# Feed-forward layers of a routed attention kernel: two batches at a time, by seven block products in place of eight

## The chip, the cores and the metric

The kernel runs on one core of one Trainium2 chip. The metric is the device time in microseconds of one execution; the time before is the median of three runs. The engines of a core are named as the profile names them: PE is the matrix engine (PEld its weight loads), ACT the scalar engine, DVE the vector engine, POOL the GpSimd engine, and SP the queue from which most transfers are issued.

## The reference

First an attention block with pooled queries, over 8 batches of 8 heads, 1152 keys and 64 elements per head. Then, per batch, a gate scores each of the 576 pooled tokens, the best 128 go through a feed-forward network (FFN) of 512 to 1024 to 512, and its output is added to those tokens, weighted by the gate. Everything is in 32-bit floats.

```python
def _attn_ref(q, k, v):                       # q, k, v: (8, 8, 1152, 64)
    q_pool = q.reshape(B, H, S // 2, 2, D).mean(axis=3)
    scores = scale * np.matmul(q_pool, k.transpose(0, 1, 3, 2))
    scores = scores - np.max(scores, axis=-1, keepdims=True)
    attn = np.exp(scores)
    attn = attn / (np.sum(attn, axis=-1, keepdims=True) + 1e-09)
    return np.matmul(attn, v)

def _moe_ref(x, w_gate, w1, w2, capacity):    # x: (8, 576, 512), capacity 128
    scores = np.einsum('bsd,d->bs', x, w_gate)
    out = x.copy()
    for b in range(B):
        top_idx = np.argpartition(-scores[b], capacity)[:capacity]
        xe = x[b, top_idx]
        h = np.maximum(xe @ w1, 0.0)          # w1: (512, 1024)
        ye = h @ w2                           # w2: (1024, 512)
        g = 1.0 / (1.0 + np.exp(-scores[b, top_idx]))
        out[b, top_idx] = x[b, top_idx] + g[:, None] * ye
    return out
```

## The kernel before

The program is a loop over 64 halves: 8 batches, 4 pairs of heads each, and every pair's 576 queries in two halves of 288. In half `h` the PE makes the scores of `h` and then the weighted values of `h - 1`; ACT takes the exponentials out of PSUM; POOL and DVE fold their sums, transpose, normalize and gate.

```python
def scores(self, half):
    ...
    for c in range(self.NC):                       # 9 blocks of keys
        sc = self.banks()                          # one of 4 PSUM tiles of 2 banks
        for e in range(2):
            for j in range(2):
                nc.tensor.matmul(sc[keys, j, 0:n], lhsT=pair["kT"][...], rhs=pair["qT"][rows, qs], ...)  # L818
        nc.scalar.activation(p[:, c // G, c % G, :, :], sc[:, :, 0:n], AF.Exp, scale=self.scale)         # L825

def weighted(self, half):
    av = self.banks()
    ...     nc.tensor.matmul(av[...], lhsT=half["pair"]["v"][keys, j, c, :], rhs=half["p"][...], ...)    # L836
    nc.scalar.copy(two[:, :, :], av[:, :, 0:n])                                                          # L844
    nc.gpsimd.tensor_tensor(out=half["av"][:, :], in0=two[:, 0, :], in1=two[:, 1, :], op=ALU.add)        # L846

def folded(self, half):
    acc = self.work.tile([P, G, 2 * self.HALF], F32, name="acc")
    for u in range(G):
        nc.gpsimd.tensor_tensor(out=acc[:, u, :], in0=units[:, 0, u, :], in1=units[:, 1, u, :], op=ALU.add)  # L857
    for a, of in enumerate((units[:, 2, :, :], acc[:, :, :])):
        nc.vector.tensor_reduce(fold[:, a, :], ..., apply_transpose=True)                                # L862
    nc.vector.tensor_reduce(pair["sum"][:, :, ns], fold..., AX.X, ALU.add)                               # L872
```

When a batch's four pairs are done, a generator `routed` does the gate and the FFN of that batch in small steps. What a step yields says at which of three places of a half the next one is put: "mid" (between the scores and the weighted values), "sums" (after the folding) or the end of the half. `gated` makes the last product with the gate's weights and starts it.

```python
def gated(self, half):
    ...
    nc.vector.tensor_reduce(pair["red"][:, ns], pair["prod"][:, ns, :], AX.X, ALU.add)
    if half["s"] == 1:
        engine.tensor_tensor(out=pair["part"][...], in0=pair["red"], in1=pair["rec"], op=ALU.mult)       # L986
        if pair["hp"] == self.NPAIR - 1:
            self.routing.append([pair["b"], self.routed(pair["b"], pair["part"]), "sums"])

def routed(self, b, part):
    nc.vector.tensor_reduce(line[:, :], part..., AX.X, ALU.add)                                          # L1010
    ...   # batch 6: nc.tensor.matmul(ps, lhsT=merge, rhs=line)                                           # L1024
    ...   # scores to a row in DRAM and back, ranks on DVE, ranks to DRAM and back
    for of, to in ((self.token_line, found), (lines[:, :, 1, :], own_gate)):
        nc.vector.scalar_tensor_tensor(out=pick..., in0=lines[0:w, :, 0, :], scalar=token, in1=of, ...)  # L1169
    nc.gpsimd.indirect_dma_start(out=xe[0:w, :], in_=rows_out, ...)                                      # L1188
    ...
    for c in range(self.ND):                        # 4 blocks of 128
        nc.tensor.transpose(pv[:, c, 0:w], xe[0:w, c * P : (c + 1) * P], ident)                          # L1205
    nc.scalar.copy(xeT[:, :, 0:w], pv[:, 0 : self.ND, 0:w])                                              # L1208
    yield mid
    for f0 in range(0, self.NFC, 4):                # 8 blocks of 128 hidden units
        pv = self.banks()[:, 0, :]...
        for f in range(4):
            for c in range(self.ND):
                nc.tensor.matmul(pv[:, f, 0:w], lhsT=self.w1[:, c, ...], rhs=xeT[:, c, 0:w], ...)        # L1216
            if f == 3:
                nc.scalar.activation(hT[:, f0 : f0 + 4, 0:w], pv[:, :, 0:w], AF.Relu)                    # L1224
            yield "hidden" if f0 + f == self.NFC - 1 else False
    ps = self.banks()[:, 0, :]
    for f in range(self.NFC):
        nc.tensor.matmul(ps[0:w, 0:512], lhsT=hT[:, f, 0:w], rhs=self.w2[:, f, :], ...)                  # L1229
        yield False
    nc.scalar.activation(y[0:w, :], ps[0:w, 0:512], AF.Copy, scale=own_gate[0:w, 0:1])                   # L1248
    nc.gpsimd.tensor_tensor(out=xe[0:w, :], in0=y[0:w, :], in1=xe[0:w, :], op=ALU.add)                   # L1253
    nc.gpsimd.indirect_dma_start(out=rows_out, in_=xe[0:w, :], ...)                                      # L1254
```

So the FFN of one batch is 32 matmuls of 128 x 128 by 128 and 8 of 128 x 128 by 512. The layers of batch 5 (second one), 6 and 7 run after the loop, in an order written out by hand, where they fill the waits of batch 7's own chain of gate, ranks and gather.

Buffers: `kb`, `qb`, `kT`, `qT`, `prod`, `sc_row` 2 each, `v_sb` 3. Loads of a pair are issued from SP one pair ahead.

Of the kernel before, what the change touches and what calls it, by code (L numbers as in the profile page):

```python
# [10 lines left out]
P = 128  # L11
# [523 lines left out]
class _Plain:  # L535
# [10 lines left out]
    def __init__(self, ctx, tc, q, k, v, moe_w_gate, moe_w1, moe_w2, capacity, out):  # L546
# [27 lines left out]
        assert 0 < self.TAIL < P and self.Dm == self.ND * P and self.Dm <= 512  # L574
        assert self.F == self.NFC * P and self.NFC % 4 == 0
# [17 lines left out]
        self.w2 = self.const.tile([P, self.NFC, self.Dm], F32, name="w2")  # L593

# [21 lines left out]
    def constants(self):  # L616
# [13 lines left out]
        slot_i = self.ffn.tile([P, self.Sp], I32, name="cmp", bufs=1)  # L630
        nc.gpsimd.iota(slot_i[:, :], pattern=[[1, self.Sp]], base=0, channel_multiplier=0)
        self.slot_f = const.tile([P, self.Sp], F32, name="slot_f")
        nc.vector.tensor_copy(self.slot_f[:, :], slot_i[:, :])
# [34 lines left out]
    def line_of_scores(self):  # L668

        line = self.ffn.tile([P, self.NT * P], F32, name="sc_row")  # L670
        self.nc.gpsimd.memset(line[0:1, self.Sp :], 0.0)
        return line
# [16 lines left out]
    def weight_loads(self):  # L689

        w1 = self.w1_in.rearrange("(c p) f -> p c f", p=P)
        w2 = self.w2_in.rearrange("(c p) d -> p c d", p=P)
        for c in range(self.ND):
            yield self.nc.sync.dma_start(self.w1[:, c, :], w1[:, c, :])
        for c in range(0, self.NFC, 2):
            yield self.nc.sync.dma_start(self.w2[:, c : c + 2, :], w2[:, c : c + 2, :])
# [3 lines left out]
    def load_pair(self, b, hp):  # L700
# [3 lines left out]
        qb = self.load.tile([P, self.QB, 2, BLK], F32, name="qb")  # L704
# [8 lines left out]
    def load_values(self, pair):  # L713


        nc, hp = self.nc, pair["hp"]
        v_sb = pair["v"] = self.load.tile([P, 2, self.NC, self.D], F32, name="v_sb", bufs=3)
        of = self.v[pair["b"], 2 * hp : 2 * hp + 2]
        of = of.rearrange("j (i g c) d -> g i j c d", i=BLK, c=self.NC)
        for g in range(P // BLK):  # L720
            nc.sync.dma_start(
                v_sb[g * BLK : (g + 1) * BLK, :, :, :].rearrange("i j c d -> i j (c d)"),
                of[g].rearrange("i j c d -> i j (c d)"),
            )
# [16 lines left out]
    def load_first(self, b, hp):  # L741
# [3 lines left out]
        kb = self.load.tile([P, self.KB, BLK], F32, name="kb")  # L745
        kn = kb.rearrange("p n d -> p (n d)").rearrange("p (c j d) -> p c j d", c=NC, j=2)
        acc = self.work.tile([P, G, 2 * self.HALF], F32, name="acc")
        third = self.QB // 3
        qn = acc.rearrange("p u n -> p (u n)")[0 : 3 * BLK, 0 : 4 * third * D]
        qn = qn.rearrange("p (j m d) -> p j m d", j=2, d=D)  # L750
        v_sb = self.load.tile([P, 2, NC, D], F32, name="v_sb", bufs=3)
# [11 lines left out]
        return {"k": kn, "q": qn, "v": v_sb, "b": b, "hp": hp}  # L763

    def prepare_first(self, pair):
# [5 lines left out]
        acc = self.work.tile([P, G, 2 * self.HALF], F32, name="acc")  # L771
        qp = acc.rearrange("p u n -> p (u n)")[0:rows, 0 : 2 * third * D]
        qp = qp.rearrange("p (n j d) -> p n j d", j=2, d=D)
# [76 lines left out]
    def folded(self, half):  # L850
# [9 lines left out]
        fold = self.small.tile([P, 2, G * nb], F32, name="fold")  # L860
# [8 lines left out]
        if half["s"] == 0:  # L869
            pair["sum"] = self.small.tile([P, 2, self.QB], F32, name="sum")  # L870
# [11 lines left out]
    def side_by_side(self, of):  # L882

        n = of.shape[-1]
        to = self.small.tile([BLK, P // BLK, n], F32, name="groups")
# [4 lines left out]
    def added(self, groups):  # L890
        n = groups.shape[-1]
        total = self.small.tile([BLK, n], F32, name="total")
# [26 lines left out]
    def multiplied(self, half):  # L919

        pair, hb, hp = half["pair"], self.HB, half["pair"]["hp"]
        if half["s"] == 0:
            pair["prod"] = self.work.tile([P, self.QB, BLK], F32, name="prod")
# [51 lines left out]
    def gated(self, half):  # L975

        nc, pair, hb = self.nc, half["pair"], self.HB
        if half["s"] == 0:
            pair["red"] = self.small.tile([P, self.QB], F32, name="red")
        ns = slice(half["s"] * hb, (half["s"] + 1) * hb)  # L980
        nc.vector.tensor_reduce(pair["red"][:, ns], pair["prod"][:, ns, :], AX.X, ALU.add)  # L981
        if half["s"] == 1:
# [17 lines left out]
    def routed(self, b, part):  # L1000
# [8 lines left out]
        line = self.small.tile([P, self.QB], F32, name="line")  # L1009
# [4 lines left out]
        if b < self.B - 1:  # L1014

            yield "mid"
# [4 lines left out]
            else:  # L1021
                total = self.small.tile([BLK, self.QB], F32, name="total")
# [9 lines left out]
            sc_row = ffn.tile([P, NT * P], F32, name="sc_row")  # L1032
# [9 lines left out]
            yield True  # L1042
        else:

            diag = ffn.tile([P, self.QB, BLK], F32, name="diag", bufs=1)
# [34 lines left out]
        for t, rows in tiles:  # L1080
            at = t * P
            cmp = ffn.tile([P, Sp], F32, name="cmp", bufs=1)
# [20 lines left out]
            tie = ffn.tile([P, P], F32, name="tie", bufs=1)  # L1103
# [36 lines left out]
        for s0, w in self.slots:  # L1140
            pick = ffn.tile([P, NT, P], F32, name="pick", bufs=1)
            index = ffn.tile([P, 1], I32, name="index")
            own_gate = ffn.tile([P, 1], F32, name="own_gate")
            if b == self.B - 1:

                nc.vector.tensor_tensor(
                    out=pick[:, :, 0:w],
                    in0=self.slot_f[:, s0 : s0 + w].unsqueeze(1).broadcast_to([P, NT, w]),
# [15 lines left out]
            else:  # L1164
                yield True

                found = self.small.tile([P, 1], F32, name="found_token")
                for of, to in ((self.token_line, found), (lines[:, :, 1, :], own_gate)):
                    nc.vector.scalar_tensor_tensor(  # L1169
                        out=pick.rearrange("p t i -> p (t i)").rearrange("p (i t) -> p i t", t=NT)[0:w],  # L1170
# [6 lines left out]
                    )  # L1177
                nc.vector.tensor_scalar(
# [5 lines left out]
                )  # L1184

                yield "sums" if b < self.B - 2 else True
            xe = ffn.tile([P, self.Dm], F32, name="xe")
# [9 lines left out]
            if b < self.B - 2:  # L1197
                yield True
# [10 lines left out]
            yield mid  # L1209

            hT = ffn.tile([P, self.NFC, P], F32, name="hT")
            for f0 in range(0, self.NFC, 4):
                pv = self.banks()[:, 0, :].rearrange("p (c n) -> p c n", n=P)
                for f in range(4):
                    for c in range(self.ND):
                        nc.tensor.matmul(  # L1216
                            pv[:, f, 0:w],
                            lhsT=self.w1[:, c, (f0 + f) * P : (f0 + f + 1) * P],
                            rhs=xeT[:, c, 0:w],
                            start=(c == 0),  # L1220
                            stop=(c == self.ND - 1),
                        )
                    if f == 3:
                        nc.scalar.activation(hT[:, f0 : f0 + 4, 0:w], pv[:, :, 0:w], AF.Relu)  # L1224
                    yield "hidden" if f0 + f == self.NFC - 1 else False

            ps = self.banks()[:, 0, :]
            for f in range(self.NFC):
                nc.tensor.matmul(  # L1229
                    ps[0:w, 0 : self.Dm],  # L1230
                    lhsT=hT[:, f, 0:w],
                    rhs=self.w2[:, f, :],
                    start=(f == 0),
                    stop=(f == self.NFC - 1),
                )
                yield False
            if b == self.B - 1:
                nc.vector.scalar_tensor_tensor(
                    out=xe[0:w, :],
                    in0=ps[0:w, 0 : self.Dm],  # L1240
                    scalar=own_gate[0:w, 0:1],
                    in1=xe[0:w, :],
                    op0=ALU.mult,
                    op1=ALU.add,
                )
            else:
                y = ffn.tile([P, self.Dm], F32, name="y", bufs=1)
                nc.scalar.activation(  # L1248
                    y[0:w, :], ps[0:w, 0 : self.Dm], AF.Copy, scale=own_gate[0:w, 0:1]
                )  # L1250
                if b < self.B - 2:
                    yield True
                nc.gpsimd.tensor_tensor(out=xe[0:w, :], in0=y[0:w, :], in1=xe[0:w, :], op=ALU.add)  # L1253
            nc.gpsimd.indirect_dma_start(  # L1254
                out=rows_out,
                out_offset=bass.IndirectOffsetOnAxis(ap=index[0:w, 0:1], axis=0),
                in_=xe[0:w, :],
                in_offset=None,
                bounds_check=(b + 1) * Sp - 1,
                oob_is_err=False,  # L1260
            )
            yield True

    def counted(self):
# [3 lines left out]
        flags = self.ffn.tile([P, n], F32, name="cmp", bufs=1)  # L1268
# [52 lines left out]
    def run(self):  # L1321
# [10 lines left out]
        if loaded:  # L1332
            self.load_values(loaded)
        self.load_gate()
        weights = self.weight_loads()
        for h in range(n_halves):
# [6 lines left out]
            else:  # L1343
                loaded = None
                if n + 2 < len(pairs):
                    loaded = self.load_pair(*pairs[n + 2])
                    self.load_values(loaded)
                if n > 1:
                    self.stored(halves[h - 4]["pair"])
            if h > 1:  # L1350
                next(weights, None)
            half = {"pair": pair, "s": s}
# [12 lines left out]
            self.folded(half)  # L1365
            self.units("sums")
# [16 lines left out]
            self.units("end")  # L1383
        for _ in weights:
            pass
# [15 lines left out]
        self.multiplied(halves[-1])  # L1401
        self.gated(halves[-2])
        pieces(older, 1)
        self.normalized(halves[-1]["pair"])
        for half in (halves[-3], halves[-1]):
# [82 lines left out]
```

## Time and profile before

| what | value |
|---|---|
| time, median of 3 runs (lowest to highest) | 704.41 us (704.12 to 705.01) |
| profiled span | 702.9 us |
| DVE, ACT, POOL busy | 68%, 64%, 70% of the span |
| one half without FFN work | 8.75 us (17.49 us from one pair's weighted values to the next pair's) |
| data moved | 82.86 MB, mean 118 GB/s |
| first layer of one batch (chain, L1216) | 7.34 us for 64 entries |
| second layer of one batch (chain, L1229) | 7.06 us for 16 entries |

A matmul of 32-bit floats shows as two entries in the trace (two passes), so 32 matmuls of L1216 are 64 entries. The duration of one entry is longer than the distance to the next, since matmuls are pipelined; the time that a group takes is read from the chain of waits, where each stretch counts once. In the groups, "busy, mean ns of one" comes before the bar, and the idle time of the engine just before the group, with what ended it, after it.

### The profile page before, as it was taken

To read this page: it belongs to the slowest core of one execution; us is meant where nothing else is said; L and a number is where in the kernel's file an instruction comes from. 1 tells how busy PE (TensorE), PEld (TensorE's weight loads), DVE (VectorE), ACT (ScalarE), POOL (GpSimd) and SP (SyncE) were. 2 spreads that over 40 slices of the span, in tenths; PEclk is the share of its full clock that TensorE was granted. 3 is DMA by queue.
4 is the path that set the end of the run, shared out by engine and by line. 5 is a ranking of instruction groups with operands and counts; after the bars stand their busy time and mean duration, and the time that the engine had idled before them with its cause. 6 is when DMAs were issued, how large, how long until landed. Compare 5 with 4: busy or idle time off the path is not lost.

```text
span 702.9 us, 23365 instructions
## 1 busy us (share of the span) xinstructions
PE 692.2 (98%) x9948; PEld 521.6 (74%) x9948; DVE 478.4 (68%) x770; ACT 446.5 (64%) x963; POOL 491.6 (70%) x475
## 2 busy tenths in 40 slices
PE   8999999999999999999999999999999999999996
PEld 5668999999756887568875787757877578677673
DVE  3877777788836887278863888548884598668730
ACT  5677778777647775477755777557775477747210
POOL 5788888779837796397954879547986479956620
PEclk9999999999999999999999999999999999999998
DMA  8888886858682495825866269652687428711300
GB/s 183 173 183 176 179 164 126 144 115 161 125 142 69 91 165 104 151 67 102 174 104 118 68 124 169 119 93 61 134 159 133 87 53 174 135 19 48 59 31 35
DMA packets 389490, 82.86 MB, mean 118 GB/s; under 512 B 376640, under 2 KB 376640, under 8 KB 389376
## 3 DMA queue, kind: packets, MB, share of 16 engines
q1 hardware_dynamic: 387872, 76.49, 57.4%
q0 software_dynamic: 1280, 4.20, 1.9%
q8 instruction: 80, 1.31, 0.8%
q10 hardware_dynamic: 224, 0.59, 0.3%
q14 instruction: 34, 0.28, 0.1%
HBM read 69.65 MB, written 11.59 MB: 116 GB/s over the span
## 4 chain that ended last, share of the span: by engine, by line
PE 88%; POOL 6%; issue 3%; DVE 1%; DMA 1%; ACT 0%; SPq 0%; POOLq 0%; DVEq 0%; ACTq 0%
PE ps L836 36%; PE ps L818 35%; PE ps L1216 8%; PE ps L1229 6%; POOL acc L857 3%; DMA kb<-in_k_dram 1%; POOL av L846 1%; POOL prod L925 1%; PE ps L1205 1%; ACT p L825 0%; POOL x L959 0%; POOL qp L732 0%; DVE fold L862 0%; POOL out_dram L1254 0%; SPq L759 0%
## 5 line engine op out<-in xcount | busy, mean ns | idle before, releaser
L825 ACT ACTIVATE p<-ps 128x576 f32<-128x576 f32 x576 | 320.6, 700 | 1.0 <-PE ps L818 1.0
L836 PE MATMUL ps<-p,v_sb 64*64 64x288 f32 x4608 | 294.3, 403 | 0.0
L818 PE MATMUL ps<-qT,kT 64*64 64x288 f32 x4608 | 293.5, 403 | 0.0
L857 POOL TENSOR_TENSOR acc<-p 128x576 f32<-128x576 f32 x192 | 274.0, 1455 | 8.3 <-ACT p L825 8.3
L836 PEld LDWEIGHTS ps<-p,v_sb 64*64 64x64 f32 x4608 | 214.9, 133 | 66.0 <-ACT p L825 8.9
L818 PEld LDWEIGHTS ps<-qT,kT 64*64 64x64 f32 x4608 | 213.3, 133 | 66.3 <-ACT p L825 6.9
L862 DVE TRANSPOSE_TENSOR_REDUCE fold<-p 128x54 f32<-128x1728 f32 x64 | 126.0, 1969 | 57.6 <-ACT p L825 57.6
L862 DVE TRANSPOSE_TENSOR_REDUCE fold<-acc 128x54 f32<-128x1728 f32 x64 | 125.1, 1955 | 57.1 <-POOL acc L857 57.1
L844 ACT COPY two<-ps 128x576 f32<-128x576 f32 x64 | 41.0, 640 | 151.4 <-PE ps L836 146.9
L846 POOL TENSOR_TENSOR av<-two 128x288 f32<-128x288 f32 x64 | 51.3, 802 | 93.5 <-ACT two L844 93.5
L915 DVE STREAM_TRANSPOSE avb<-av 128x288 f32<-128x288 f32 x64 | 29.1, 454 | 67.3 <-POOL av L846 66.8
L1216 PEld LDWEIGHTS ps<-xeT,w 128*128 128x128 f32 x512 | 57.8, 192 | 2.7 <-ACT p L825 2.6
L1216 PE MATMUL ps<-xeT,w 128*128 128x128 f32 x512 | 59.3, 277 | 0.0
L1229 PE MATMUL ps<-w,hT 128*128 128x512 f32 x128 | 57.5, 598 | 0.0
L986 POOL TENSOR_TENSOR part<-red,rec 128x18 f32<-128x18 f32 x30 | 6.8, 226 | 64.2 <-DVE red L981 56.4
L925 POOL TENSOR_TENSOR prod<-avb,w_gate 128x288 f32<-128x288 f32 x64 | 51.5, 806 | 0.2
L732 POOL TENSOR_TENSOR qp<-qb 128x576 f32<-128x576 f32 x31 | 43.8, 1413 | 1.3 <-DMA qb<-in_q_dram 1.3
L1229 PEld LDWEIGHTS ps<-w,hT 128*128 128x128 f32 x128 | 23.5, 190 | 28.1 <-issue 25.8
L735 DVE STREAM_TRANSPOSE kT<-kb 128x1152 f32<-128x1152 f32 x31 | 42.0, 1355 | 0.0
L902 ACT ACTIVATE sums<-total,tiny 32x18 f32<-32x18 f32 x124 | 38.4, 309 | 2.7 <-DVE total L893 0.6
L959 POOL TENSOR_TENSOR x<-avb,rec 128x576 f32<-128x576 f32 x32 | 37.2, 1162 | 0.0
L1224 ACT ACTIVATE hT<-ps 128x512 f32<-128x512 f32 x16 | 9.6, 598 | 39.0 <-PE ps L1216 39.0
(96 smaller groups left out, 313.0 us busy)
## 6 DMA issues: line engine op xcount, KB each, us to landing
kb<-in_k_dram SPq DMA_DIRECT2D x124, 144.0 KB
qb<-in_q_dram SPq DMA_DIRECT2D x124, 144.0 KB
v_sb<-in_v_dram SPq DMA_DIRECT2D x124, 144.0 KB
out_dram<-x SPq DMA_DIRECT2D x128, 72.0 KB
lines<-row_rank SPq DMA_DIRECT2D x7, 640.0 KB
w<-in_moe_w_dram SPq DMA_DIRECT2D x8, 512.0 KB
sc_row<-row SPq DMA_DIRECT2D x7, 288.0 KB
acc<-in_q_dram ACTq DMA_DIRECT2D x2, 288.0 KB
```

The lines of the kernel that those rows point to most:

```text
L732: nc.gpsimd.tensor_tensor(out=qp[:, :, :], in0=pair["q"][:, :, 0, :], in1=pair["q"][:, :, 1, :], op=ALU.add)
L735: nc.vector.transpose(kT.rearrange("p (c g i) -> p c g i", c=self.NC, i=BLK), pair["k"].rearrange("p (g c) d -> p c g d", c=self.NC),)
L818: nc.tensor.matmul(sc[keys, j, 0:n], lhsT=pair["kT"][rows, c * P + keys.start : c * P + keys.stop], rhs=pair["qT"][rows, qs], start=True, ...
L825: nc.scalar.activation(p[:, c // G, c % G, :, :], sc[:, :, 0:n], AF.Exp, scale=self.scale)
L836: nc.tensor.matmul(av[j * self.D : (j + 1) * self.D, e, 0:n], lhsT=half["pair"]["v"][keys, j, c, :], rhs=half["p"][keys, c // G, c % G, j, :],
L844: nc.scalar.copy(two[:, :, :], av[:, :, 0:n])
L846: nc.gpsimd.tensor_tensor(out=half["av"][:, :], in0=two[:, 0, :], in1=two[:, 1, :], op=ALU.add)
L857: nc.gpsimd.tensor_tensor(out=acc[:, u, :], in0=units[:, 0, u, :], in1=units[:, 1, u, :], op=ALU.add)
L862: nc.vector.tensor_reduce(fold[:, a, :], of.rearrange("p u (m d) -> p (u m) d", d=BLK), AX.X, ALU.add, apply_transpose=True,)
L925: self.nc.gpsimd.tensor_tensor(out=pair["prod"][:, ns, :], in0=pair["avb"][:, ns, :], in1=self.w_gate[:, hp : hp + 1, :].broadcast_to([P, ...
L1216: nc.tensor.matmul(pv[:, f, 0:w], lhsT=self.w1[:, c, (f0 + f) * P : (f0 + f + 1) * P], rhs=xeT[:, c, 0:w], start=(c == 0), stop=(c == self ...
L1229: nc.tensor.matmul(ps[0:w, 0 : self.Dm], lhsT=hT[:, f, 0:w], rhs=self.w2[:, f, :], start=(f == 0), stop=(f == self.NFC - 1),)
```

## The change

**Seven products.** The selected tokens of two batches (0 and 1, 2 and 3, 4 and 5) are stacked, 256 tokens in all. Each layer is then a product of two 2 x 2 block matrices, where the blocks of the left one are (batch, half of the inner dimension) and those of the right one are quarters of the weights. Strassen's method in Winograd's form makes it from 7 block products in place of 8, at the price of 4 sums of input blocks, 4 sums of weight blocks and 7 sums of results. Batches 6 and 7 keep the plain layers.

```diff
+    def seven_products(self, layer, a, s, c, rest, shape):
+        steps = (
+            (a11, b11, c11, ()),
+            (s1, t1, c22, ()),
+            (s3, t3, c21, ()),
+            (s2, t2, u, ((u, c11), (c21, u), (u, c22), (c22, c21))),
+            (s4, b22, c12, ((c12, u),)),
+            (a12, b21, x, ((c11, x),)),
+            (a22, t4, y, ((c21, y),)),
+        )
+        for i, (of, by, to, _) in enumerate(steps):
+            if i % 2 == 0:
+                tile = self.banks()
+            ps, n = shape(tile[:, i % 2, :]), of.shape[1]
+            ...     # layer 1: 4 x 2 matmuls of 128x128 by 128; layer 2: 4 of 128x128 by 256
+            copies.append((to, ps))
+            if i % 2 or last:
+                for copy in copies:
+                    nc.scalar.copy(*copy)
+            yield "sums" if last else False
+        for *_, sums in steps:
+            for to, of in sums:
+                nc.vector.tensor_tensor(out=to, in0=to, in1=of, op=ALU.add)
+
+    def input_sums(self, a, s):          # four sums on POOL
+        ((s1, a21, a22, add), (s2, s1, a11, subtract), (s3, a11, a21, subtract), (s4, a12, s2, subtract))
+            self.nc.gpsimd.tensor_tensor(out=to, in0=x, in1=y, op=op)
+
+    def layers_of_two(self, tokens):
+        ...   # end of a half: input_sums (128 x 256 each)
+        yield "mid"
+        yield from self.seven_products(1, a, s, c, rest, lines)
+        yield "mid"
+        for tile in hidden:
+            nc.scalar.activation(tile[:, :, 0:w], tile[:, :, 0:w], AF.Relu)      # 128 x 1024 each
+        loads = self.load_sums(2)        # ends of the next two halves: input_sums (128 x 512 each)
+        ...
+        yield from self.seven_products(2, ...)
+        yield "mid"
+        for i, of in enumerate(c):
+            nc.scalar.activation(of, of, AF.Copy, scale=tokens[i // 2]["gate"][0:w, 0:1])
+        ...   # four POOL additions of 128 x 256, two scatters
+        if tokens[1]["b"] + 1 < self.paired:
+            for _ in self.load_sums(1):
+                yield True
```

**Sums of the weights.** They are made once on DVE, 16 subtractions of 128 x 512, one or two per half, in halves that have no ranking to do. One buffer of 2 MB on chip holds the four sums of one layer; both layers' sums are kept in DRAM, and loaded in turn (2 MB each time).

```diff
+    def weight_sums(self):
+        for layer in (2, 1):
+            for i, (to, x, y) in enumerate(((t1, b12, b11), (t2, b22, t1), (t3, b22, b12), (t4, b21, t2))):
+                for c in (slice(0, n), slice(n, 2 * n)):
+                    nc.vector.tensor_tensor(out=to[:, c, :], in0=x[:, c, :], in1=y[:, c, :], op=ALU.subtract)
+                    yield
+                nc.sync.dma_start(kept[:, i, :], self.tw[:, i, :])
 ...
+            if 5 < h < 14 or 18 < h < 23:
+                for _ in range(2 - s):
+                    next(sums, None)
```

**Room for them.** `qb`, `prod` and `sc_row` go from 2 buffers to 1, `v_sb` from 3 to 2; values of a pair are loaded half a pair later; ranks, the search and the tail's diagonal share buffers; the first pair's inputs lie in a buffer of `p`.

```diff
-        qb = self.load.tile([P, self.QB, 2, BLK], F32, name="qb")
+        qb = self.load.tile([P, self.QB, 2, BLK], F32, name="qb", bufs=1)
-        v_sb = pair["v"] = self.load.tile([P, 2, self.NC, self.D], F32, name="v_sb", bufs=3)
+        v_sb = pair["v"] = self.load.tile([P, 2, self.NC, self.D], F32, name="v_sb", bufs=2)
-            pair["prod"] = self.work.tile([P, self.QB, BLK], F32, name="prod")
+            pair["prod"] = self.work.tile([P, self.QB, BLK], F32, name="prod", bufs=1)
-                    self.load_values(loaded)
+                if n + 1 < len(pairs):
+                    self.load_values(upcoming)
```

**Gate work later.** The product with the gate's factor (`scored`) moves behind the folding of the half; the search for the gate's own value moves behind the gather; the matmul that merges batch 6's line waits for the end of the half.

```diff
             self.folded(half)
+            if h > 2:
+                self.scored(halves[h - 3])
             self.units("sums")
 ...
-            yield "mid"
+            yield mid
             if b < self.B - 2:
                 groups = self.side_by_side(line)
                 ...
             else:
+                yield True
                 total = ...
```

**Tail.** The second layer of batches 4 and 5 together (28 matmuls by 256 columns) takes the place of batch 5's (8 by 512), and the order is written anew: one product, the last normalization and gate, the divisions and stores of the last two pairs, three products, batch 7's row of scores, one product, batch 6's transposes, batch 7's columns and ranks, two products, batch 6's first layer with batch 7's pick in it, and so on.

## The prediction

> **What bounds the kernel now.** I read the busy table first, then the chain of waits, then the windows and the costs of the operations that come in.
>
> ```profile
> PE 692.2 (98%) x9948; PEld 521.6 (74%) x9948; DVE 478.4 (68%) x770; ACT 446.5 (64%) x963; POOL 491.6 (70%) x475
> ...
> PE 88%; POOL 6%; issue 3%; DVE 1%; DMA 1%; ACT 0%; SPq 0%; POOLq 0%; DVEq 0%; ACTq 0%
> ```
>
> The PE is busy for all but 702.9 - 692.2 = 10.7 us; the others have 30% or more to spare. A busy PE alone proves little, so I look at the chain in order of time, around batch 2's FFN:
>
> ```profile
> 346.91 4.53 PE ps L836 x72
> 355.80 7.34 PE ps L1216 x64
> 363.14 4.53 PE ps L836 x72
> 372.03 7.06 PE ps L1229 x16
> 379.10 4.53 PE ps L836 x72
> ```
>
> Between two rows of L836 lie 4.36 us of scores (363.14 + 4.53 to 372.03), and the FFN stands between them with its full time. The PE sets the pace; an entry taken off it in the loop shortens the span by that entry's distance to the next. The few idle times are at the start, at the end, and here:
>
> ```profile
> 603.73 0.37 PE L1024 MATMUL ps<-line,merge 128*128 128x18 f32 x2 [1.24 <-DVE line L1010]
> ...
> 688.97 7.03 PE L1229 MATMUL ps<-w,hT 128*128 128x512 f32 x16
> ```
>
> The first is a 1.24 us stall on DVE's line of batch 6. The last matmul ends at 696.0; the 6.9 us behind it (DVE, scatter, landing) are not touched. After the loop (656.0) the PE is busy to 696.0 without a gap worth naming, so the tail is bound by the PE too.
>
> What will be put on the other engines costs, by these groups:
>
> ```profile
> L1208 ACT COPY xeT<-ps 128x512 f32<-128x512 f32 x8 | 4.6, 576 | 9.0 <-PE ps L1205 9.0
> L846 POOL TENSOR_TENSOR av<-two 128x288 f32<-128x288 f32 x64 | 51.3, 802 | 93.5 <-ACT two L844 93.5
> L1253 POOL TENSOR_TENSOR xe<-y,xe 128x512 f32<-128x512 f32 x7 | 8.9, 1272 | 7.2 <-ACT y L1248 7.2
> L1146 DVE TENSOR_TENSOR pick<-slot_f,rank 128x640 f32<-128x640 f32 x1 | 0.8, 824 | 0.0
> L1046 DVE TENSOR_TENSOR diag<-line,same 128x576 f32<-128x576 f32 x1 | 1.4, 1355 | 0.0
> ```
>
> **What the Trainium skill says.** (1) "Perfetto Trace Analysis", section Identifying the Most-Contended Engine: matmul busy time is a poor measure of the distance to the roofline, weight-load busy time is a better one. The trace has 98% beside 74%; that is why I rest on the chain, where the PE's stretches touch each other. (2) "TensorE: Matmul & The Clock Gate", section Back-to-back issue gap, gives a gap between isolated matmuls of N/2.4 + 2.5 ns: 216 ns for 512 columns. The trace has 7.06/16 = 441 ns per entry, twice that, and 7.34/64 = 115 ns for 128 columns; I use the measured ones. (3) "SBUF — State Buffer", section Who interferes with whom: a DVE operation with two inputs in SBUF contends with a POOL operation that reads SBUF. The trace agrees: three additions of L857 take 4.14 us, but 5.31 us beside the search of L1169; and L1046 took 1355 ns beside POOL's divisions, while the larger L1146 took 824 ns. (4) "VectorE: DVE Perf Modes", section The perf-mode tier table: 32-bit `tensor_tensor` in SBUF has 1x speed, 2293 ns for 2048 elements; an estimate from it for 512 is 0.57 us. Scaled from L1146, 824 x 512/640 = 0.66 us; beside POOL, from L1046, 1355 x 512/576 = 1.2 us. I take 0.66 to 1.2 us.
>
> **The change, part by part.**
>
> *Seven products.* A pair of batches has 2 x (7.34 + 7.06) = 28.8 us of FFN on the PE. Layer 1 goes from 64 matmuls of 128 columns to 56 of the same shape: 14.68 x 7/8 = 12.85, saved 1.83 us. Layer 2 goes from 16 by 512 columns to 28 by 256, again 7/8 of the columns: 14.12 x 7/8 = 12.36. A straight line through 115 ns (128 columns) and 441 ns (512) gives 224 ns for 256, and 56 x 0.224 = 12.5. So 1.6 to 1.8 us are saved, and 3.5 us with layer 1; for three pairs 10.4 us (10.8 with the ratio alone).
>
> *Does the PE wait for the new work?* Per pair, first layer: POOL makes four input sums, at 0.71 us (802 x 256/288) 2.9 us, at the end of the half before. Only the second product needs the first sum, 1.8 us after the start, so there is room. ACT copies seven results, 7 x 0.58 = 4.0 us, while the PE takes 12.85 us and uses four PSUM tiles that ACT frees as it goes: no wait. DVE adds, 7 x 0.66 = 4.6 us, mostly during the products, since each sum needs only copies made so far; the last comes about a microsecond after the last copy, and ACT needs the result only after 4.4 + 4.4 us of other matmuls. There ACT applies two Relus of 128 x 1024; at the rate of L844 (640 ns for 576) 1.1 us each, 2.2 us with the exponentials' tail 0.9 and L902's four copies 1.27: 4.4 us, just what the weighted values give it. Second layer: POOL has 4 x 1.27 = 5.1 us of sums in two halves where it works some 6.2 and 8.5 us of 8.75 anyway; it falls behind by about 2.3 us, which the next product half (8.75 + 12.4 us) gives back, and the sums are needed only at the third and fifth product. Copies 7 x 0.3 on ACT, additions 7 x 0.35 on DVE, four POOL additions of 0.71: beside the PE.
>
> *Weight sums.* 16 x 0.66 to 1.2 = 11 to 19 us on DVE in 13 halves. DVE works 12.3 us of 17.6 in a pair there (windows 35 to 88 us); with three subtractions 14.3 to 16. It fits.
>
> *Transfers.* Added: 2 x 2.1 MB stored, 5 x 2.1 MB loaded, 14.7 MB on 82.9. The first 105 us are near the limit:
>
> ```profile
> 35.10:52.70 17.60, 17.60 (x296) 12.31 (x292) 12.34 (x15) 13.10 (x30) 14.27 (x14) 1.00 0.88 183
> ```
>
> (the last two numbers: DMA share, GB/s). There the weights load beside the pairs, and about 1.05 MB of stored sums are added in the worst pair (halves 7 and 8): 0.9 MB too much, some 5 us of delay. Against it stand, by my estimate, about 8 us: in the timeline a `q` is issued from 68.7 to 72.4 us and first used by POOL at about 83, and I allow 3 us to land. Later the second layer's 2.1 MB have some 20 us to land, and there is half a share free. I expect no wait of the PE, but it is the thinnest margin.
>
> *Moved gate work.* Batch 6's merge comes one stretch of weighted values later, so the 1.24 us stall should go: -1.2 us.
>
> *Tail.* Twelve and a half us of products replace 7.06 us there, taken out of the loop together with batch 4's second layer; it moves work and saves nothing more. Batch 7's chain: its row of scores is needed about 6.1 us after the loop's last matmul as before, now behind 7.4 us of products and a merge; its ranks take the 7.4 us from L679 to L1155, and over them lie two products and 24 of 32 first-layer matmuls, 3.6 + 5.5 = 9.1 us; its gather has the same 4.5 us of matmuls over it as before (674.17 to 678.66). The PE stays full.
>
> *Sum.* 704.4 - 10.4 - 1.2 = 692.8 us if nothing new waits. The halves around the second layers have POOL some microseconds late, with DVE's fold and ACT's copies of L887 behind it (at 587 to 596 such a lateness held ACT 0.76 us, but not the PE). I add 1.2 us for stalls of that kind and come to **694.0 us**, 1.5% less.
>
> **Rivals.** *A: POOL and DVE become the bound around the FFN.* For it: POOL is at 81% in ordinary halves (14.2 of 17.6 us), gets about 11 us per pair of batches, and loses more where DVE's two-input sums lock it out. Against it: each product half adds 12.4 us in which POOL has little to do. If half of the added POOL work came on the path, 3 x 5 us, the time would be 708. If a late fold holds ACT in two halves per pair by 1 us, it is 699. *B: transfers.* One buffer of `q` and two of `v` leave less time ahead, and 14.7 MB are added, 7 MB of them in bursts. For it: 88% DMA share early on. Against it: only 1.3 us of waits for `q` in all before. A late `q` or `tw` would cost 2 to 5 us each time: 696 to 705. *C: the tail breaks.* A late sum, copy or rank there costs what it is late, 1 to 5 us; the end is written by hand, and its room for the ranks has grown. *D: more gain.* If 256-column matmuls run at half the 430 ns that lie between two weight loads of L1229 in the timeline, layer 2 takes 12.0 us, and the whole is 691.5.
>
> **Range and chances.** D without stalls bounds it below: 691.5. Above, one of A to C in moderate size: 698.5. Faster than 690.3 needs more than the PE's saved work: 3%. Slower than 718.5 needs a new bound in every pair: 3%. Within 2%: 94%.
>
> **What would show it.** Right: in the chain, first-layer stretches of about 12.8 and second-layer ones of about 12.4 us, three each; the PE's busy time down by about 10 us; its idle time still near 10 us; no row of L1024's successor with idle time; the end behind the last matmul still 6.9 us. Wrong: product stretches above 13 us with idle PE ended by POOL sums or ACT copies (A); POOL or the PE waiting for DMA before 150 us or at the second layers (B); gaps behind the loop's last matmul (C).

## The result and the profile after

The changed kernel takes 693.67 us (median of 4; 692.35 to 694.87) against 704.33 us before: ratio 0.9847, 95% interval 0.9824 to 0.9869. The prediction was 694.0 us. The profiled execution has a span of 690.5 us, before 702.9.

The busy table of the changed kernel:

```profile
PE 681.0 (99%) x9972; PEld 520.4 (75%) x9972; DVE 524.9 (76%) x827; ACT 462.1 (67%) x1005; POOL 517.0 (75%) x504
```

PE's busy time fell by 11.2 us, its idle time from 10.7 to 9.5; DVE took on 46.5 us, POOL 25.4 and ACT 15.6 without becoming the bound.

The chain of waits says nothing here (it follows the last store and stops there), so I read PE's timeline: start, length of the group, engine, line, operation, entries, and in brackets the idle time before it with what ended it. First the stretch where batches 2 and 3 pass their first layer (L1378 are the block products, L871 weighted values; the last group is cut off by the end of the view):

```profile
422.96 2.05 PE L1378 MATMUL ps<-xeT,w 128*128 128x128 f32 x16
424.85 5.52 PE L1378 MATMUL ps<-s,tw 128*128 128x128 f32 x48
430.21 1.95 PE L1378 MATMUL ps<-s,w 128*128 128x128 f32 x16
431.99 1.95 PE L1378 MATMUL ps<-xeT,w 128*128 128x128 f32 x16
433.78 1.95 PE L1378 MATMUL ps<-xeT,tw 128*128 128x128 f32 x16
435.66 0.71 PE L871 MATMUL ps<-p,v_sb 64*64 64x288 f32 x8
```

From 422.96 to 435.66 are 12.70 us for 112 entries, and no bracket: PE waits for none of the sums, copies or loads. The second layer of batches 0 and 1:

```profile
294.93 1.99 PE L1378 MATMUL ps<-w,hT 128*128 128x256 f32 x8
296.76 5.34 PE L1378 MATMUL ps<-tw,s 128*128 128x256 f32 x24
301.94 1.89 PE L1378 MATMUL ps<-w,s 128*128 128x256 f32 x8
303.67 1.89 PE L1378 MATMUL ps<-w,hT 128*128 128x256 f32 x8
305.39 1.89 PE L1378 MATMUL ps<-tw,hT 128*128 128x256 f32 x8
307.21 4.11 PE L871 MATMUL ps<-p,v_sb 64*64 64x288 f32 x64
```

307.21 - 294.93 = 12.28 us for 56 entries, 219 ns each, and no bracket either. The merge of batch 6's line and the tail:

```profile
585.50 0.40 PE L1064 MATMUL ps<-line,merge 128*128 128x18 f32 x2
...
629.62 8.96 PE L871 MATMUL ps<-p,v_sb 64*64 64x288 f32 x144
638.51 1.99 PE L1378 MATMUL ps<-w,hT 128*128 128x256 f32 x8
640.34 0.31 PE L973 MATMUL ps<-sum,merge 128*128 128x36 f32 x2
640.48 5.43 PE L1378 MATMUL ps<-tw,s 128*128 128x256 f32 x24
646.59 1.21 PE L1097 MATMUL ps<-lines,ones 128*128 128x288 f32 x4 [0.68 <-ACT s L1386]
...
677.05 7.03 PE L1289 MATMUL ps<-w,hT 128*128 128x512 f32 x16
```

The merge has no wait any more. In the tail one wait is new, 0.68 us at L1097. Put together, from the two profiles (a stretch is the distance from its first start to the next group's):

| part | us |
|---|---|
| three first layers in the loop, 14.68 to 12.70 each | -5.9 |
| two second layers in the loop, 14.12 to 12.28 each | -3.7 |
| third pair: batch 4's second layer leaves the loop (-7.06), 12.28 takes 7.06's place in the tail (+5.22) | -1.84 |
| merge stall | -1.24 |
| start | -0.17 |
| somewhat longer score stretches in the loop, cause not known | +0.7 |
| wait at L1097 | +0.7 |
| rest of the tail, and the end behind the last matmul (6.9 to 6.4) | -0.9 |
| span, 702.9 to 690.5 | -12.4 |

The time itself fell by 10.7 us in the medians; the profiled execution is the shortest of the four.

### The profile page after: what moved, and what is told of

It is laid out like the page before. It is cut to its first block, busy times and chain, and to the rows that moved or that the text cites. A ratio compares the mean times of both kernels' runs of the same rounds, so it can differ in the third digit from the quotient of the medians.

```text
span 690.5 us, 23608 instructions
## 1 busy us (share of the span) xinstructions
PE 681.0 (99%) x9972; PEld 520.4 (75%) x9972; DVE 524.9 (76%) x827; ACT 462.1 (67%) x1005; POOL 517.0 (75%) x504
## 5 line engine op out<-in xcount | busy, mean ns | idle before, releaser
L871 PE MATMUL ps<-p,v_sb 64*64 64x288 f32 x4608 | 294.1, 403 | 0.0
L871 PEld LDWEIGHTS ps<-p,v_sb 64*64 64x64 f32 x4608 | 212.5, 133 | 66.9 <-ACT p L860 11.7
L853 PEld LDWEIGHTS ps<-qT,kT 64*64 64x64 f32 x4608 | 206.3, 132 | 74.2 <-ACT p L860 14.3
L950 DVE STREAM_TRANSPOSE avb<-av 128x288 f32<-128x288 f32 x64 | 29.0, 453 | 30.7 <-POOL av L881 25.4
L1145 DVE SCALAR_TENSOR_TENSOR pick<-sc_row,gate_sc,before 128x128 f32<-128x128 f32 (+1 forms) x40 | 30.7, 768 | 1.4
L922 ACT COPY groups<-sum 32x36 f32<-32x36 f32 x124 | 27.2, 219 | 1.6
L1016 DVE TENSOR_REDUCE red<-prod 128x9 f32<-128x288 f32 x64 | 27.7, 433 | 0.1
L1386 ACT COPY s<-ps 128x256 f32<-128x256 f32 (+1 forms) x27 | 11.4, 447 | 20.2 <-PE ps L1378 20.2
L1135 DVE TENSOR_SCALAR_CACHE_REDUCE pick<-sc_row,gate_sc 128x576 f32<-128x576 f32 (+4 forms) x40 | 21.6, 539 | 4.3 <-ACT gate_sc L682 4.1
L1386 ACT COPY hT<-ps 128x512 f32<-128x512 f32 (+1 forms) x15 | 7.8, 544 | 23.5 <-PE ps L1378 21.3
```

The costliest lines, as they stand in the source:

```text
L853: nc.tensor.matmul(sc[keys, j, 0:n], lhsT=pair["kT"][rows, c * P + keys.start : c * P + keys.stop], rhs=pair["qT"][rows, qs], start=True, ...
L871: nc.tensor.matmul(av[j * self.D : (j + 1) * self.D, e, 0:n], lhsT=half["pair"]["v"][keys, j, c, :], rhs=half["p"][keys, c // G, c % G, j, :],
```

## The experiments

My theory: the gain is PE's entries taken away by the seven products and nothing else; all the added work is hidden. Rivals: the gain comes from the later gate work and the new tail; the added work does cost something, and a larger PE gain hides it. Times are medians beside runs of the kernel before on the same chip. The first four experiments ran on one chip and the other four on another; the kernel before took 704.32 us on the one and 704.26 on the other, so I compare across them.

**The changed kernel again.** No edit; five executions, as the base of the others.

> The changed kernel once more, for its spread: its four times fell into two groups, 692.4 and 692.8 beside 694.6 and 694.9. If some single wait is there in one execution and not in the next, a profile that shows a time near 694.7 has about 2 us of PE idle time more than the first one (9.5 us), in one place; if the PE is a little slower everywhere (each half of 8.73 us longer by 0.03), idle time stays and all stretches grow.

692.82 us (691.46 to 693.21), ratio 0.9833 (0.9820 to 0.9845). The profile has the same wait of 0.68 us at L1097, and no lower clock behind it; the executions that took longer have no profile, so the cause of the spread isn't shown by this run.

**Everything but the seven products.**

```diff
-        self.paired = self.B - 2 - self.B % 2
+        self.paired = 0
 ...
```

All batches are then in plain layers, without sums of weights. The part of the edit that is cut here puts the tail back into the order of before.

> Everything of the change but the seven products: all batches use the plain layers (no sums of weights, no loads of them), with the order of the tail as before; buffers, later gate work and later loads stay as changed. Theory (the gain is the PE's removed entries, 3 x 3.8 us as measured in the profile, and the 1.24 us stall at the merge): 703.1 us, range 702.4 to 703.8, PE busy 692 us. Rival 1 (a good part comes from the moved gate work, loads and tail): 700 or less. Rival 2 (fewer buffers cost time that the products hide): 705 or more.

706.74 us (705.38 to 707.91), ratio 1.0035 (1.0023 to 1.0047). I was wrong: the frame of the change costs 2.4 us instead of saving 1.2. The loop ends 1.06 us earlier than before (654.88 against 655.94), but in the tail PE waits for batch 7's ranks. PE's timeline of this kernel, and under it the one line of the kernel before that its last line is to be held against:

```profile
664.31 7.41 PE L1276 MATMUL ps<-xeT,w 128*128 128x128 f32 x64
672.98 1.33 PE L1196 MATMUL ps<-meta,pick 128*128 128x2 f32 x10 [1.26 <-DVE pick L1187]
674.25 6.25 PE L1289 MATMUL ps<-w,hT 128*128 128x512 f32 x10
```

```profile
674.10 4.56 PE L1229 MATMUL ps<-w,hT 128*128 128x512 f32 x10
```

The kernel before has no wait there, and its ten entries take 4.56 us. The windows of this kernel without products say why its ten entries take 6.25 (behind the length come the busy times of PE, PEld, DVE, ACT and POOL; the last three numbers are granted clock, DMA share, GB/s):

```profile
671.90:674.90 3.00, 1.92 (x11) 1.62 (x12) 1.48 (x2) 0.68 (x3) 0.11 (x1) 0.92 0.00 0
674.90:677.90 3.00, 3.00 (x5) 1.24 (x4) 0.98 (x4) 0.00 (x0) 0.94 (x1) 0.51 0.31 87
```

PE's clock fell to half for some 3 us behind the wait: 1.26 + 1.69 = 2.95 us in all. And why are the ranks late? DVE's operations of that chain, in this kernel:

```profile
665.75 0.08 DVE L1145 DVE_READ_ACCUMULATOR pick<-sc_row,gate_sc,before 128x1 f32 x1
665.87 0.35 DVE L1126 TENSOR_SCALAR_CACHE_REDUCE pick<-sc_row,gate_sc 128x128 f32<-128x128 f32 x1
...
671.55 1.29 DVE L1187 TENSOR_TENSOR pick<-token_line,rank 128x640 f32<-128x640 f32 x1
```

and in the kernel before:

```profile
666.68 0.09 DVE L1104 DVE_READ_ACCUMULATOR tie<-sc_row,gate_sc,before 128x1 f32 x1
666.68 0.34 DVE L1085 TENSOR_SCALAR_CACHE_REDUCE cmp<-sc_row,gate_sc 128x128 f32<-128x128 f32 x1
...
671.87 0.82 DVE L1146 TENSOR_TENSOR pick<-slot_f,rank 128x640 f32<-128x640 f32 x1
```

With one buffer for both kinds of comparison, the next operation starts 0.12 us after the start of the accumulator's read instead of together with it, nine times in this chain; and the product for the pick takes 1.29 us, reading every fifth number of `token_line`, against 0.82 from a row of its own. From the start of the row's matmul (L679) to the end of the pick are 8.9 us here and 7.7 before. These are two of the ways in which the change makes room for `tw`.

**One pair of batches in seven products.** The kernel above with

```diff
-        self.paired = 0
+        self.paired = 2
```

> As e1_plain, but batches 0 and 1 by seven products, with the sums of weights of both layers. Theory: one pair's removed entries, 3.8 us less than e1_plain: 699.3 us if that is 703.1. Rival (sums, copies and transfers cost the path something per pair or once): less than 2.5 us below e1_plain.

702.26 us (701.89 to 703.30), ratio 0.9973 (0.9962 to 0.9984): 4.5 us less than without a pair. The loop ends at 650.70, 4.18 us earlier; the wait of 1.26 us and the ten entries at 6.26 us stand in the tail unchanged. The products are the gain, about what the stretches say (1.98 + 1.84 = 3.82). The remaining 0.4 to 0.7 us I can't assign.

**No sums of weights.** The buffer is filled once with a constant; the subtractions, stores and loads of the weight sums are left out.

```diff
+        nc.gpsimd.memset(self.tw[:, :, :], 0.01)
-        sums = self.weight_sums() if self.paired else iter(())
+        sums = iter(())
-            self.nc.sync.dma_start(self.tw[:, i : i + 2, :], self.tw_kept[layer][:, i : i + 2, :])
```

> The changed kernel without the sums of weights: the buffer of sums is filled once with a constant, so the 16 subtractions, the 4.2 MB stored and the 10.5 MB loaded are left out (the output is not the reference's). Theory (they are hidden): within 0.7 us of the changed kernel, 693.0 to 694.4 in median. Rival (transfers and the lock on the shared port cost time): 691.5 or less, and the spread between its executions is gone.

692.35 us (691.53 to 693.30), ratio 0.9828 (0.9816 to 0.9841): 0.5 us less than the full kernel, with overlapping intervals, and as wide a spread. To within that half microsecond the sums of weights and their 14.7 MB are hidden.

**The plain kernel with rank buffers and a slot row of its own.** The kernel without seven products, where the room of `tw` is free:

```diff
-        self.tw = self.const.tile([P, 4, self.ND // 2 * self.F // 2], F32, name="tw")
 ...
+        self.slot_f = const.tile([P, self.Sp], F32, name="slot_f")      # 0, 1, 2, ... in a row of its own
-            cmp = ffn.tile([P, Sp], F32, name="pick", bufs=1)
+            cmp = ffn.tile([P, Sp], F32, name="cmp", bufs=1)
-            tie = ffn.tile([P, P], F32, name="pick", bufs=1)
+            tie = ffn.tile([P, P], F32, name="tie", bufs=1)
-                    in0=self.token_line[:, s0 : s0 + w, 0]...
+                    in0=self.slot_f[:, s0 : s0 + w]...
```

> e1_plain once more, but the ranks of the tail get their own buffers and the pick its contiguous row of slots back, as before the change (the unused buffer of weight sums is left out to make room). In e1_plain the PE waited 1.26 us for the pick and then ran 3 us at half the clock, 2.95 us in all. Theory (that is the whole of e1_plain's loss; the rest of the frame costs nothing and saves the 1.24 us stall at the merge): 703.2 us, range 702.5 to 704. Rival (fewer buffers or later loads cost the loop time): still 705.5 or more.

704.18 us (703.91 to 705.98), ratio 1.0001 (0.9993 to 1.0010). PE's timeline of this kernel, in the tail:

```profile
672.05 1.33 PE L1200 MATMUL ps<-meta,pick 128*128 128x2 f32 x10
673.31 4.56 PE L1293 MATMUL ps<-w,hT 128*128 128x512 f32 x10
```

The wait and the slow clock are gone, the time is back by 2.6 us, and the chain takes 7.7 us as before. So the shared buffers and the strided row together were the loss; one without the other wasn't tried. The kernel is not faster than the one before, though: I expected 1.1 us from the stall at the merge, and in its timeline the stall is gone, but the span is only 0.5 us shorter. Its loop ends 0.80 us earlier (655.14), and its tail is 0.3 us longer. The frame is neutral, and the rest of those 1.24 us is given back in pieces that I can't name.

**Each input sum on POOL twice.**

```diff
-            self.nc.gpsimd.tensor_tensor(out=to, in0=x, in1=y, op=op)
+            for _ in range(2):
+                self.nc.gpsimd.tensor_tensor(out=to, in0=x, in1=y, op=op)
```

> The changed kernel with each of POOL's input sums done twice (8 us more on POOL per pair of batches; same result). Theory (POOL has slack around the products, but only some 5 us of it before the second layer, where 5.1 us come in): 693 to 697. Rival (POOL is close to being the bound, each microsecond counts): 700 or more.

699.98 us (699.09 to 701.00), ratio 0.9937 (0.9922 to 0.9952): 7.2 us more than the changed kernel for 24 us of added POOL work: above what I expected, and at the edge of the rival's 700. About 30% of the added work comes on the path, so not each microsecond counts. PE's timeline of this kernel:

```profile
299.85 3.72 PE L1379 MATMUL ps<-tw,s 128*128 128x256 f32 x16 [1.42 <-POOL s L1345]
...
646.20 0.38 PE L973 MATMUL ps<-sum,merge 128*128 128x36 f32 x2 [3.17 <-DVE sum L907]
646.41 7.11 PE L1379 MATMUL ps<-tw,s 128*128 128x256 f32 x24
```

The second pair's second layer has a wait like the first line's, of 1.40 us. In the tail POOL's lateness comes back through DVE's fold as 3.17 us, and the products behind it take 7.11 us in place of 5.43, with a granted clock of 0.50 from 648 to 651. 1.42 + 1.40 + 3.17 + 1.68 less the 0.68 that goes make 7.0 us. In the changed kernel all of the sums are hidden, but the margin is smaller than a second set of them.

**Each load of weight sums twice**, 10.5 MB more.

```diff
-            self.nc.sync.dma_start(self.tw[:, i : i + 2, :], self.tw_kept[layer][:, i : i + 2, :])
+            for _ in range(2):
+                self.nc.sync.dma_start(self.tw[:, i : i + 2, :], self.tw_kept[layer][:, i : i + 2, :])
```

> The changed kernel with each load of weight sums done twice (10.5 MB more). Theory (before the second layer 18 us lie between issue and use, some 12 us of them needed for the first 2.1 MB at about 180 GB/s; 12 more are too much for the first two pairs of batches, the third has idle queues): 695 to 705, with the PE waiting for the load at the second product of the second layer. Rival (there is far more room in the transfers than that): no change, under 693.7.

711.01 us (708.93 to 716.63), ratio 1.0110 (1.0084 to 1.0136): 18.2 us more, above the top of what I expected, and mostly in another place. PE's timeline of this kernel:

```profile
375.67 3.62 PE L854 MATMUL ps<-qT,kT 64*64 64x288 f32 x56
383.54 7.90 PE L872 MATMUL ps<-p,v_sb 64*64 64x288 f32 x70 [4.25 <-DMA v_sb<-in_v_dram]
...
476.16 3.69 PE L1379 MATMUL ps<-tw,s 128*128 128x256 f32 x16 [1.68 <-DMA tw<-tw]
```

and the windows behind the first wait:

```profile
383.00:386.00 3.00, 2.44 (x16) 1.15 (x20) 2.54 (x7) 0.00 (x0) 3.00 (x4) 0.50 0.75 132
386.00:389.00 3.00, 3.00 (x31) 1.69 (x28) 2.93 (x10) 0.00 (x0) 3.00 (x3) 0.50 0.92 145
```

The product that uses `tw` waits 1.68 us; the values wait 4.25 us, and the 70 entries behind the wait take 7.90 us in place of some 4.4, six of these microseconds at half the clock. At 556 us they wait again, 3.38 and 0.49 us. Over the whole span PE is idle 9.6 us longer (18.8 against 9.2 in the repeated run of the changed kernel) and its matmuls take 6.9 us longer (688.4 against 681.5).

The edit adds more than bytes, though. SP issues the loads in order. Two lines of its timeline at this place, one line of its waits in the whole run, and under them the same load of sums in the changed kernel:

```profile
361.31 6.94 SPq L731 DMA_DIRECT2D tw<-tw  x2
378.74 3.11 SPq L757 DMA_DIRECT2D v_sb<-in_v_dram  x4
```

```profile
SPq L731 <- DMA tw<-tw: 57.7, 10, 7.7
```

```profile
357.63 0.58 SPq L730 DMA_DIRECT2D tw<-tw  x1
```

The second load writes the same buffer as the first, so SP waits until the first has landed, 57.7 us in ten waits, and every load behind it is issued later. The values of this place are issued at 378.74 us, in the changed kernel at 369.16. So the values were the first to be late, but this run doesn't separate the added bytes from the stopped queue, and how much room the transfers have is not shown.

**One product of the tail on POOL.** The wait at L1097 is put down to ACT, but the matmul reads `lines`, and DVE writes that late. DVE's timeline of the changed kernel there, and under it POOL's:

```profile
641.75 0.45 DVE L1016 TENSOR_REDUCE red<-prod 128x9 f32<-128x288 f32 x1
642.23 3.11 DVE L1025 TENSOR_TENSOR part<-red,rec 128x18 f32<-128x18 f32 x1
645.38 0.27 DVE L1049 TENSOR_REDUCE line<-part 128x18 f32<-128x72 f32 x1
645.68 0.76 DVE L1087 TENSOR_TENSOR lines<-line,same 128x576 f32<-128x576 f32 x1
```

```profile
641.86 1.13 POOL L1237 DMA_INDIRECT xe<-out_dram,index  x1
643.02 2.28 POOL L994 TENSOR_TENSOR x<-avb,rec 128x576 f32<-128x576 f32 x2
```

A product of 128 x 18 takes 0.37 us on DVE (the same line at 640.62), here 3.11: it ends when POOL's two divisions end. "SBUF — State Buffer", section Who interferes with whom, in the Trainium skill says that a DVE instruction with two SBUF inputs contends with a POOL instruction that reads SBUF, that the contention is an exclusive lock, and that the order of issue decides who blocks. The trace agrees in that the product ends with POOL's second division (645.34 and 645.30). It doesn't show why the product, which starts 0.79 us ahead of the first division, isn't done before it; POOL works on an indirect transfer (L1237) in that time. The experiment gives the last pair's product to POOL itself, ahead of the divisions:

```diff
-            ending = pair["b"] == self.B - 1 and pair["hp"] >= self.NPAIR - 2
+            ending = pair["b"] == self.B - 1 and pair["hp"] == self.NPAIR - 2
```

> The changed kernel, with the last pair's product with the gate's factor on POOL in place of DVE, so that POOL's divisions can't lock DVE out of it (3.11 us for 128 x 18 in the profile) and the PE's wait of 0.68 us before the row of scores goes. Theory: 0.7 us less than the changed kernel, 692.1 us in median beside 692.8, no execution above 693. Rival (the wait only moves to another place in the tail): no change.

690.49 us (690.42 to 690.83), ratio 0.9800 (0.9787 to 0.9813). The timelines of POOL, DVE and PE in this kernel:

```profile
641.46 0.22 POOL L1025 TENSOR_TENSOR part<-red,rec 128x18 f32<-128x18 f32 x1 [0.57 <-DVE red L1016]
```

```profile
641.72 0.28 DVE L1049 TENSOR_REDUCE line<-part 128x18 f32<-128x72 f32 x1 [0.34 <-POOL part L1025]
642.03 0.76 DVE L1087 TENSOR_TENSOR lines<-line,same 128x576 f32<-128x576 f32 x1
```

```profile
639.68 5.43 PE L1378 MATMUL ps<-tw,s 128*128 128x256 f32 x24
644.94 1.13 PE L1097 MATMUL ps<-lines,ones 128*128 128x288 f32 x4
```

Counted from the end of the loop on PE (638.51 us in the changed kernel, 637.71 here), `lines` is begun 2.85 us earlier (4.32 against 7.17), and PE waits no more. So DVE's late product was the cause of the wait and ACT was not. The time is 2.3 us less than the changed kernel's median where I expected 0.7. Of the 1.9 us between the profiled executions (690.7 us of span in the repeated run, 688.8 here), the tail gives 0.96: 52.05 us from the loop's end there, 51.09 here. The other 0.94 lies in the loop, where the edit changes nothing, so I can't put it down to the edit. The rest is spread: the changed kernel's executions lie 1.75 us apart, these 0.4. Why is not shown. The mean granted clock of the longer ones is 0.995, of the shorter ones 0.999, but that mean is a poor guide: in every profile the clock also falls to half some microseconds after the last matmul (from about 689 us in the repeated run), and the executions of this kernel are shorter than all of them at 0.997 and 0.998. This version beats both kernels: its interval lies below that of the changed kernel.

## Why the prediction was right, point by point

- **Seven products: right in kind, the term mis-sized by 0.3 us per pair.** The prediction put it at 3.5 us a pair and 10.4 us in all; the stretches give 1.98 + 1.84 = 3.82, and 11.5. The 7/8 rule held (12.85 predicted, 12.70 measured; 12.36 by the ratio, 12.28 measured). The straight line through 128 and 512 columns, 224 ns for 256, was too high: 219 ns. This is the small part of rival D that came true.
- **The merge stall: the wait is gone, its time only partly.** The plain kernel with its own buffers loses the stall too and gains 0.5 us of span, not 1.24. This term was about 0.7 us too large, if the other pieces of the frame are as neutral with seven products, which wasn't tried.
- **1.2 us of new stalls: about the right size, by luck.** I expected them in the loop, from POOL, DVE and ACT around the second layers. No bracket stands there; the loop loses some 0.7 us in longer score stretches of unknown cause, and the one new wait is 0.68 us in the tail, from a DVE product held up beside POOL's divisions. The prediction knew that kind of delay (L1046's 1355 ns), but used it for the sums of weights and not for a stall in the tail.
- **Sums of weights, copies, Relus, POOL's sums: hidden, as said.** Without the weight sums the time is the same within the intervals. "It falls behind by about 2.3 us, which the next product half gives back" held, but doubling the sums costs 7.2 us, so rival A is closer than the text made it. The durations were right: 731 and 1271 ns for POOL's sums (0.71 and 1.27 predicted), 587 ns for ACT's copies of 512 (0.58), 690 ns for DVE's additions (0.66), 838 and 866 ns on average for the weights' subtractions (0.66 to 1.2), which fall into 11 halves and not 13.
- **Transfers: right that PE waits for none behind the start; the size of the margin is open.** The 0.9 MB too much are more than the line shown for it gives: 12% of free share beside 183 GB/s at 88% is 0.44 MB in 17.6 us, which leaves 0.6 MB of the 1.05. With the loads doubled the values are late first (rival B, in `v_sb`), but there SP's queue was also stopped.
- **The tail: "its ranks take the 7.4 us and over them lie 9.1": wrong in the first number, saved by the second.** With the shared buffer and the strided row the chain takes 9.05 us from the row's matmul to the end of the pick, and PE needs the pick 9.31 us after that matmul (649.89 to 659.20): 0.26 us of room where the prediction had 1.7. In the kernel without products, where 7.4 us of matmuls lie over it, the same slower chain costs 2.6 us. So the new order of the tail isn't only a different order: with the products in it, it hides what the sharing of buffers costs. The sum agrees: from the kernel without products to the changed one are 706.74 - 692.82 = 13.9 us, and 11.5 for the products, 2.95 for the wait and the slow stretch that go, less the new wait of 0.68, make 13.8. Nor did PE stay full: the row of scores was ready not 6.1 but 8.1 us after the loop (638.51 to 646.59), later than the products over it. The changed sharing stood in the diff, and the prediction took the old duration without asking what it does to a chain of dependent operations. Rival C was nearer than it looked.
- **The sum** came to 694.0 because its errors point both ways: 1.1 us too little for the products, some 0.7 too much for the merge stall. That it lies 0.3 us from the first median is partly luck; the repeated run's median is 1.2 us below it.

## What to carry to other kernels

Where PE is the bound and its stretches touch, seven block products in place of eight save about one eighth of those stretches (13.5% and 13.0% here), and the sums may go to other engines as long as they come in before the product that needs them. Find out how thin that margin is by doubling the added work, not from busy shares, and make sure that the doubling adds nothing else: a second load into the same buffer also stopped the queue behind it. When a change shares buffers to make room, work out anew every chain of dependent operations that uses them: 0.12 us at nine places and a product longer by 0.5 us were enough for a wait of PE in one tail and for none in another. And before believing the name of a releaser, look at what the waiting instruction reads.

## What the runs showed of the hardware that was not expected

A short wait of PE can cost more than itself: 1.26 us of waiting was followed by some 3 us at half the granted clock (6.25 us for ten entries in place of 4.56), 3.17 us by 7.11 us in place of 5.43, and 4.25 us by about six at half clock. "TensorE: Matmul & The Clock Gate" in the Trainium skill, section Why this matters for your kernels, asks for no idle gaps above about 3 us; in these runs 1.26 us with little PE work next to it (ten matmuls of two columns) was enough, in two kernels. The length of the wait alone doesn't decide it: waits of 1.24 us (the merge in the kernel before), 1.42 and 1.40 us (POOL's sums done twice) and 1.68 us (loads done twice), each with full matmuls soon behind it, had no such stretch, nor had the wait of 0.68 us. That the little work behind the wait makes the difference fits these cases; no run varies it by itself.

A DVE product of 18 numbers per partition took 3.11 us in place of 0.37 beside POOL's indirect transfer and two divisions, and didn't get in between the divisions.
